# Streaming-window attention with folded feed-forward weights: the casting queue's gate one piece earlier, paired copies of fold sums, and new numbers in the planner

## The chip, the cores and the metric

The kernel runs on 1 core of one Trainium2 chip. The metric is the device time of one execution in microseconds. Before the change it is 201.57 us, the median of three runs (201.42 to 201.92).

The engines are named as in the profile: PE is TensorE (PEld its weight loads), DVE is VectorE, ACT is ScalarE, POOL is GpSimd and SP is SyncE. SP and POOL issue nearly all transfers here: SP plain copies and transposing copies, POOL those that cast from float32 to bfloat16 on the way.

## What is computed

Attention with 4 sink keys and a window of 128 keys over 4 batches, 8 heads, 768 positions and 64 dimensions, followed by a gated feed-forward block whose last two matrices follow each other with nothing between them:

```python
scores = scale * q @ k.transpose(0, 1, 3, 2)
keep = is_sink | in_window            # 4 sinks; 0 <= i - j < 128
a = softmax(where(keep, scores, -1e9))
x = (a @ v)  as [3072, 512]
out = ((x @ w1) * (x @ w2)) @ w3 @ w_out
```

`w1` and `w2` are 512 x 1024, `w3` is 1024 x 1024 and `w_out` is 1024 x 512.

## The kernel before

**Folding.** The product `w3 @ w_out` doesn't depend on the tokens. The kernel works it out once, as `w3o`, in 8 row blocks of 128: `fold_w3` transposes a row block of `w3` on PE (line 403) and DVE copies the result (line 408), `fold_mm` multiplies it with `w_out` on PE (line 433) in four steps of two column blocks each, and ACT copies the finished sum of 128 x 512 from PSUM into `w3o` (line 437). For row blocks 0 to 3 the sums of a pair (0 and 1, 2 and 3) are the two halves of one PSUM tile `ph`, taken from the pool that the attention scores use too (`ps_sc`, two buffers); row blocks 4 to 7 have a tile `pw` each.

**Loading.** Nine pieces of `w3` and `w_out` of 512 KB each come uncast over SP's queue, straight away (`raws`, line 155), into memory that is used for other things later; DVE or ACT casts each of them (line 413). All else comes through POOL's queue: for batch 0 the keys, queries and values, one row block of 128 positions at a time (line 108), two more pieces of `w3` (line 115), and `w1` and `w2` in quarters (line 111). This queue is held back: POOL first copies one column of the piece `casts[hold - 1]` into `spent` (line 190), so it can't issue a load before that piece has landed. In POOL's order the copy stands after the masks and before all loads. With `hold = 6` it is the sixth piece. The loads of batches 1 to 3 are emitted later, when the planner has all folding done.

**Attention.** For each batch, keys and queries are transposed: on PE for batches 0 and 1 (line 200, copied by DVE in line 202), by transposing copies on SP's queue for batches 2 and 3 (line 207). PE works out scores (lines 256 and 277), ACT the exponentials (lines 261 and 281), DVE applies the mask, PE multiplies with the values (lines 309 and 346), DVE divides, and the result is transposed into `xT`, on PE or, for batches 2 and 3, by copies on SP's queue (line 373).

**Feed-forward.** `gate` multiplies `xT` with `w1` and with `w2` on PE (line 386); ACT copies the first product (line 393) and DVE multiplies the second into it (line 390). `project` multiplies with `w3o` (line 444), ACT copies (line 448) and SP writes the result out (line 451). A batch's gates come in chunks of 256 tokens for batch 0 and of 384 for the others, 8 column blocks each.

**The order of the work.** The order of instructions on PE, ACT, DVE and SP is made in Python before anything runs. Each piece of work is a `task` with a priority, a cost for each stage, and the tasks, loads and PSUM buffers that it waits for. `landings` works out when each load lands: `RAW` is when SP's queue begins to move data, `DGE` the time from POOL's issue to the first data, the third number of an entry the lag from the last data to the landing. `service` gives, for each load of POOL's queue, the time that POOL takes to issue it and the time that its data take. `landings` counts `spent` as passed 0.3 us after the held piece lands, keeps eight of POOL's loads in flight, and shares the DMA engines by fixed numbers while both queues have work: for small attention loads, 0.79 of full speed to the uncast pieces and 0.13 to the others. A loop then picks the next instruction of each engine by these times. `PACE` is the shortest time, for each batch, between the starts of two pairs of score units. `keep_busy` puts matmuls on zeros (line 458) where PE would otherwise stand in the first 40 us of the plan. Once made, each engine's order is fixed: an instruction whose input is late holds up all that stand behind it on its engine.

Of the kernel before, what the change touches and what calls it, by code (L numbers as in the profile page):

```python
# [21 lines left out]
def kernel(  # L22
# [13 lines left out]
    nc = tc.nc  # L36
# [14 lines left out]
    KFF = DF // P  # L51

    CHUNKS = [[(256 * i, 256 * i + 256) for i in range(3)]] + [[(0, 384), (384, 768)]] * (B - 1)
    XPOSE = (2, 3)
# [23 lines left out]
    w3o = wp.tile([P, KFF, DM], BF16, name="w3o")  # L78
# [39 lines left out]
    def load(what, *i):  # L118
# [9 lines left out]
        else:  # L128
            for dst, src in ((w1_sb, moe_w1), (w2_sb, moe_w2)):
# [3 lines left out]
    raws = [("w3", 0, 0, "dve"), ("wo", 0, 0, "act"), ("w3", 2, 0, "dve"), ("wo", 2, 0, "act"),  # L133
            ("w3", 4, 0, "dve"), ("wo", 4, 0, "act"), ("w3", 0, 1, "dve"), ("wo", 6, 0, "act"),
            ("w3", 2, 1, "dve")]
    hold = 6

    order = [("qkv", 0, 0, 1), ("w3", 4, 1, 2), ("qkv", 0, 1, 2), ("w3", 6, 0, 2), ("qkv", 0, 2, 3),
             ("qkv", 0, 3, 4), ("w12", 0, 1), ("w12", 1, 2), ("w12", 2, 3), ("w12", 3, 4), ("qkv", 0, 4, 5),
             ("qkv", 0, 5, 6), ("qkv", 1, 0, 6), ("qkv", 2, 0, 6), ("qkv", 3, 0, 6)]  # L140
# [258 lines left out]
    def fold_w3(i, j0, j1):  # L399

        tp = ps_mm.tile([P, j1 - j0, P], BF16, tag="mm", name="tp3")
        for j in range(j0, j1):
            nc.tensor.transpose(tp[:, j - j0, :], w3_sb[:, i, j * P:(j + 1) * P], ident)
        yield
        if i not in w3T:
            w3T[i] = (flat((kN, qN)[i - 4][1], "k s")[:, 2048:3072].rearrange("p (k n) -> p k n", n=P)
                      if i in (4, 5) else work.tile([P, KFF, P], BF16, tag="w3t", bufs=4, name="w3t"))
        nc.vector.tensor_copy(w3T[i][:, j0:j1, :], tp[:])
        yield
# [6 lines left out]
    held = {}  # L416
    FM = [[(0, 2), (2, 4), (4, 6), (6, KFF)] for i in range(KFF)]

    def folded(i):
        return ("fm", i, len(FM[i]) - 1)  # L420

    def fold_mm(i, j0, j1):

        if i >= 4:
            if j0 == 0:
                held[i] = ps_mm.tile([P, DM], FP32, tag="mm", name="pw")
            po = held[i][:]
        else:
            if i % 2 == 0 and j0 == 0:
                held[i // 2] = ps_sc.tile([P, 2, DM], FP32, tag="sc", name="ph")  # L430
            po = held[i // 2][:, i % 2, :]
        for j in range(j0, j1):
            nc.tensor.matmul(po, w3T[i][:, j, :], wo_sb[:, j, :],  # L433
                             start=(j == 0), stop=(j == KFF - 1))
        yield
        if j1 == KFF:
            nc.scalar.copy(w3o[:, i, :], po)  # L437
        yield

    def project(b, m, n0, n1):  # L440

# [20 lines left out]

    def service(what, *i):
        if what == "qkv":
            return [(0.87, 0.845 + (1.2 if i[0] in XPOSE and x != "v" else 1.3 if (x, *i) == ("v", 0, 4, 5) else 0.0), [(x, i[0], kb)])
                    for kb in range(i[1], i[2]) for x in "kqv"]
        if what == "w3":
            return [(0.75, 1.3 * (i[2] - i[1]), [("w3", i[0], h) for h in range(i[1], i[2])])]
        if what == "wo":
            return [(0.81, 0.65 * (i[1] - i[0]), [("wo", x, 0) for x in range(i[0], i[1], 2)])]  # L470
        return [(0.8, 1.34 * (i[1] - i[0]), [(w,) + (n,) for n in range(i[0], i[1])]) for w in ("w1", "w2")]

    def landings(RAW=2.0, POOL=3.0, DGE=1.6, RAMP=(0.33, 0.64, 0.66, 0.9)):

        queues = {"sp": [(RAW, 1.31, 1.0, [("raw",) + x[:3]]) for x in raws],
                  "pool": [(gen, us, 1.9, keys) for x in order for gen, us, keys in service(*x)]}
        left = {n: [us for _, us, _, _ in q] for n, q in queues.items()}
        at = {n: 0 for n in queues}
        landed, issue, ready, now = [], POOL, [], 0.0
        while any(at[n] < len(q) for n, q in queues.items()):  # L480
            while len(ready) < len(queues["pool"]) and (len(ready) < 8 or len(landed) > len(ready) - 8) \
                    and at["sp"] >= hold:
                if not ready and hold:
                    issue = max(issue, arrive[("raw",) + raws[hold - 1][:3]] + 0.3)
                if len(ready) >= 8:
                    issue = max(issue, landed[len(ready) - 8])
                issue += queues["pool"][len(ready)][0]
                ready.append(max(5.8, issue + DGE))
            busy = [n for n, q in queues.items() if at[n] < len(q)
                    and now >= (q[at[n]][0] if n != "pool" else ready[at[n]] if at[n] < len(ready) else 1e9)]  # L490
            small = queues["pool"][at["pool"]][3][0][0] if "pool" in busy else ""
            for n in busy:
                i = int(now - RAW) if now >= RAW else 0
                share = 1.0 if len(busy) == 1 else 0.5 if small not in "kqv" else 0.79 if n == "sp" else 0.13
                left[n][at[n]] -= 0.02 * share * (RAMP[i] if i < len(RAMP) else 1.0)
                if left[n][at[n]] <= 0.0:
                    lag, keys = queues[n][at[n]][2:]
                    for key in keys:
                        arrive[key] = now + lag
                    if n == "pool":  # L500
                        landed.append(now + lag)
                    at[n] += 1
            now += 0.02

    landings()

    tasks = {}
# [3 lines left out]
    def task(name, prio, gen, stages, after=(), loads=(), ring=None, started=(),  # L511
             half=False, slots=1, paced=False):
        tasks[name] = dict(name=name, prio=prio + nudge.get(name, 0.0), gen=gen, stages=stages, after=list(after),
                           loads=list(loads), ring=ring, started=list(started), half=half,
                           slots=slots, paced=paced)
# [6 lines left out]
    def need(what, i, h):  # L522
        key = (what, i // 2 * 2, h)
        return ([("c",) + key], []) if key in raw_keys else ([], [key])

    for i in range(KFF):
        for h in range(2):
            j0, j1 = 4 * h, 4 * h + 4
            needs = [need("w3", i, x) for x in range(j0 // 4, j1 // 4)]
            task(("t3", i, h), 100 + i + (5 if i < SPLIT and h else 0), fold_w3(i, j0, j1),  # L530
                 [("pe", 0.055 * (j1 - j0)), ("dve", 0.05 + 0.075 * (j1 - j0))],
                 [x for a, _ in needs for x in a], [x for _, a in needs for x in a],
                 started=[("t3", i, 0)] if i >= SPLIT and h else [folded(i - SPLIT)] if i >= SPLIT else [], ring="mm")
        for h, (j0, j1) in enumerate(FM[i]):
            last = j1 == KFF
            begin = i < 4 and i % 2 == 0 and h == 0
            needs = [need("wo", x, 0) for x in range(j0, j1, 2)]
            task(("fm", i, h), 100.5 + i + (5 if i < SPLIT and j0 >= 4 else 0) + 0.1 * h, fold_mm(i, j0, j1),
                 [("pe", 0.216 * (j1 - j0))] + ([("act", 0.6)] if last else []),
                 [("t3", i, 1 if j0 >= 4 else 0)] + ([("fm", i, h - 1)] if h else [])  # L540
                 + [x for a, _ in needs for x in a],
                 [x for _, a in needs for x in a],
                 "sc" if begin else "mm" if i >= 4 and h == 0 else None,
                 started=[("fm", i - 1, 0)] if i < 4 and not begin and h == 0 else [])
            if last and (i % 2 or i >= 4):
                tasks["fm", i, h]["frees"] = ("fm", i if i >= 4 else i - 1, 0)
# [70 lines left out]
    for b in range(B):  # L617
        for c, (t0, t1) in enumerate(CHUNKS[b]):
            last_t = (t1 - 1) // 256
            us = 0.01 + 0.65 * (t1 - t0) / 384  # L620
# [21 lines left out]
    MARGIN = {"av": 0.3}  # L642

    YIELD = {"g": 0.0, "av": 0.0, "sc": 0.4, "tdk": 1.5, "tdq": 1.5}
    PACE = [0.0, 3.2, 4.5, 5.0]
    last_sc = 0.0
    START, WARM_UNTIL = 1.2, 40.0
    BACKLOG = 1.6
# [12 lines left out]
    def pe_pick():  # L661
        best = None
        for k in tasks.values():
# [16 lines left out]
            if k["paced"]:  # L680
                busy = max(0.0, free["act"] - free["pe"]) + sum(q[2] for q in queue["act"])
                est = max(est, free["pe"] + busy - BACKLOG, last_sc + (PACE[k["name"][1]]))
            wait = est - free["pe"]
# [32 lines left out]
    while len(done) < len(tasks):  # L716
# [4 lines left out]
        for k in tasks.values():  # L721
            e, us = k["stages"][0]
# [5 lines left out]
        pe = pe_pick()  # L728
# [9 lines left out]
        if e == "pe":  # L738
# [8 lines left out]
            us = k["stages"][0][1]  # L747
# [5 lines left out]
        else:  # L753
            q = picks[e]
            queue[e].remove(q)
            us, k = q[2], q[3]
# [37 lines left out]
```

## Time and profile before

| | us |
|---|---|
| median of three runs | 201.57 |
| the profiled execution | 200.9 |
| its span, first to last instruction | 199.2 |
| DVE busy | 111.1 |
| ACT busy | 107.9 |
| POOL busy | 75.6 |

The granted PE clock was 0.998 of full speed over the span. A row of the timeline gives the start in us from the start of the span, the length, engine, line, operation, output and inputs, the number of instructions merged into the row, and in brackets how long the engine stood before it and what released it. A row of the chain of waits gives start, length and what. A row of a table by stretches gives the stretch, its length, and for each engine its busy time and number of instructions, then the granted clock, the DMA share and GB/s.

### The profile page before, as it was taken

The page shows a single profiled execution, that of the slowest core. Times are in us where ns is not written, and L with a number is a line of the kernel's source. Part 1 is how long each engine was busy: PE and PEld are TensorE (multiplying, and loading weights), DVE is VectorE, ACT ScalarE, POOL GpSimd, SP SyncE. Part 2 cuts the span into 40 slices and gives each one's busy share as a digit, 9 for nine tenths or more (in the row PEclk, how much of TensorE's full clock was granted, in tenths as well). Part 3 has the DMA queues.
Part 4 walks back from the last instruction along what each step waited for, and adds up shares of the span by engine and source line. Part 5 has one row for each costly group of instructions (what it writes and reads, how often), then busy time and mean ns, then how long its engine had stood idle before and what let it go on. Part 6 is the DMA issues. An engine that isn't in the chain of part 4 may idle for free.

```text
span 199.2 us, 4550 instructions
## 1 busy us (share of the span) xinstructions
PE 192.8 (97%) x1815; PEld 119.2 (60%) x1815; DVE 111.1 (56%) x262; ACT 107.9 (54%) x181; POOL 75.6 (38%) x102
## 2 busy tenths in 40 slices
PE   7999899999999999999999999999999999999993
PEld 2445465889866887665656655665664465554442
DVE  5555487756589778677768656767751044440000
ACT  2234576843767877866775656766622433333332
POOL 5149978679899954545374200000000000000000
PEclk9999999999999999999999999999999999999999
DMA  4999999999999999999999999960505410002333
GB/s 148 382 389 152 173 159 192 195 169 153 155 150 180 198 162 111 148 172 164 131 153 147 131 156 179 219 64 0 56 0 161 155 56 2 0 0 104 143 142 141
DMA packets 105301, 28.35 MB, mean 142 GB/s; under 512 B 95168, under 2 KB 99776, under 8 KB 105280
## 3 DMA queue, kind: packets, MB, share of 16 engines
q0 software_dynamic: 79648, 12.33, 87.2%
q1 hardware_dynamic: 25488, 15.60, 38.0%
q8 instruction: 14, 0.23, 0.5%
q10 hardware_dynamic: 144, 0.13, 0.2%
q14 instruction: 7, 0.06, 0.1%
HBM read 29.36 MB, written 6.29 MB: 179 GB/s over the span
## 4 chain that ended last, share of the span: by engine, by line
PE 85%; DMA 8%; POOL 3%; SPq 1%; DVE 1%; ACT 1%; issue 0%
PE pg L386 43%; PE po L444 21%; PE av L346 6%; PE sc L256 5%; DMA ab<-in_moe_w_out_dram 4%; DMA qN<-in_q_dram 3%; PE tp L200 3%; PE pw L433 2%; SPq L155 1%; POOL kN L108 1%; PE xt L362 1%; PE av L309 1%; PE sp L237 1%; PE sc L277 1%; POOL qN L108 1%; ACT ex L281 1%
## 5 line engine op out<-in xcount | busy, mean ns | idle before, releaser
L386 PE MATMUL pg<-xT,w_sb 128*128 128x384 bf16 (+1 forms) x576 | 92.4, 308 | 0.0
L386 PEld LDWEIGHTS <-w_sb 128*128 128x128 bf16 x576 | 52.7, 98 | 24.7 <-issue 1.6
L390 DVE TENSOR_TENSOR ab<-a_sb,pg 128x384 bf16<-128x384 f32 (+1 forms) x72 | 36.6, 509 | 36.5 <-PE pg L386 31.8
L393 ACT COPY a_sb<-pg 128x384 f32<-128x384 f32 (+1 forms) x72 | 32.0, 445 | 35.0 <-PE pg L386 17.3
L444 PE MATMUL po<-w3o,ab 128*128 128x512 bf16 (+1 forms) x200 | 43.1, 371 | 0.0
L261 ACT ACTIVATE ex<-sc 128x1024 bf16<-128x1024 f32 (+1 forms) x40 | 37.4, 963 | 5.7 <-PE sc L256 4.1
L444 PEld LDWEIGHTS <-ab 128*128 128x128 bf16 x200 | 19.1, 98 | 20.6 <-issue 0.5
L448 ACT COPY w_sb<-po 128x512 f32<-128x512 f32 (+1 forms) x25 | 14.2, 569 | 25.9 <-PE po L444 25.8
L108 POOL DMA_DIRECT2D qN<-in_q_dram x24 | 22.2, 923 | 11.2 <-DMA vN<-in_v_dram 8.6
L265 DVE TENSOR_TENSOR am<-ex,maskt 128x1024 bf16<-128x1024 bf16 (+1 forms) x40 | 25.4, 645 | 1.3 <-ACT ex L261 1.0
L108 POOL DMA_DIRECT2D kN<-in_k_dram x24 | 22.4, 933 | 7.6 <-DMA qN<-in_q_dram 4.6
L108 POOL DMA_DIRECT2D vN<-in_v_dram x24 | 21.7, 904 | 6.4 <-DMA kN<-in_k_dram 5.0
L353 DVE TENSOR_TENSOR xn<-av,rec 128x256 bf16<-128x256 f32 x40 | 17.0, 425 | 1.4
L346 PE MATMUL av<-vN,am 128*128 128x65 bf16 x296 | 16.2, 193 | 0.0
L346 PEld LDWEIGHTS <-am 128*128 128x128 bf16 x296 | 14.0, 97 | 2.3
L350 DVE RECIPROCAL rec<-av 128x4 f32<-128x4 f32 x40 | 7.1, 179 | 10.4 <-PE av L346 10.3
L256 PE MATMUL sc<-kqT 64*128 64x128 bf16 (+1 forms) x216 | 11.6, 238 | 0.0
L202 DVE COPY kqT<-tp 128x1024 bf16<-128x1024 bf16 x12 | 8.3, 691 | 5.4 <-PE tp L200 5.3
L346 PE MATMUL av<-vs,es 128*128 128x130 bf16 x56 | 11.1, 220 | 0.0
L256 PEld LDWEIGHTS <-kqT 64*128 64x128 bf16 x216 | 6.9, 94 | 4.0 <-issue 3.2
L281 ACT ACTIVATE ex<-sc 128x1024 bf16<-128x1024 f32 x7 | 7.2, 1031 | 2.9 <-PE sc L277 2.8
L433 PE MATMUL ph<-wo_sb,w3t 128*128 128x512 bf16 x32 | 7.9, 380 | 0.7 <-ACT w3o L437 0.3
(68 smaller groups left out, 138.2 us busy)
## 6 DMA issues: line engine op xcount, KB each, us to landing
out_dram<-w_sb SPq DMA_DIRECT2D x23, 256.0 KB, 2.2
kN<-in_k_dram POOLq DMA_DIRECT2D x24, 128.0 KB, 7.9
qN<-in_q_dram POOLq DMA_DIRECT2D x24, 128.0 KB, 8.1
vN<-in_v_dram POOLq DMA_DIRECT2D x24, 128.0 KB, 7.9
w_sb<-in_moe_w_dram POOLq DMA_DIRECT2D x9, 256.0 KB, 8.3
ab<-in_moe_w_dram SPq DMA_DIRECT2D x3, 512.0 KB, 6.5
ab<-in_moe_w_out_dram SPq DMA_DIRECT2D x3, 512.0 KB, 7.4
kN<-in_moe_w_dram SPq DMA_DIRECT2D x1, 512.0 KB, 9.4
```

The lines of the kernel that those rows point to most:

```text
L108: nc.gpsimd.dma_start(out=dst, in_=rows(src, b, kb))
L256: nc.tensor.matmul(sc[:, e, c:c + n], kT[b][hp, r, kb * P:(kb + 1) * P], qT[b][hp, r, qb * P:qb * P + n], start=True, stop=True)
L261: nc.scalar.activation(ex[:, :, c0:], sc[:, :, c0:], ACTF.Exp, scale=scale)
L265: nc.vector.tensor_mul(am[:, :, c0:], ex[:, :, c0:], mk)
L346: nc.tensor.matmul(o, lhs, rhs, start=(n == 0), stop=(n == len(todo) - 1), skip_group_check=True)
L353: nc.vector.tensor_mul(xns[b, t][:, :, r, :, :], av[:, :, :, 0:D], rec[:].to_broadcast([P, 2, 2, D]))
L386: nc.tensor.matmul(pg[:], w_sb[:, kk, dt * P:(dt + 1) * P], xT[b][:, kk, tk], start=(kk == 0), stop=(kk == NP - 1))
L390: nc.vector.tensor_mul(ab[b][:, dt, tk], gate_a.pop((b, c, dt))[:], pg[:])
L393: nc.scalar.copy(a_sb[:], pg[:])
L433: nc.tensor.matmul(po, w3T[i][:, j, :], wo_sb[:, j, :], start=(j == 0), stop=(j == KFF - 1))
L444: nc.tensor.matmul(po[:], ab[b][:, kk, m * P:(m + 1) * P], w3o[:, kk, n0:n1], start=(kk == 0), stop=(kk == KFF - 1))
L448: nc.scalar.copy(o_sb, po[:])
```

## The change

The gate `spent` reads the fifth uncast piece, not the sixth. For row blocks 0 to 3 the copy of a finished sum is done once for a pair: the even row block has no copy, and the odd one copies both halves of the tile, 128 x 1024, to `w3o`; its last step is made to wait for the last step of the even row block in the plan. Row blocks 4 to 7 are as before. The rest are numbers of the planner: the issue time of batch 0's attention loads, the extra time of one of them, the start and the lag of POOL's loads, the cost of the paired copy, and the pacing of batches 1 to 3.

```diff
-    hold = 6
+    hold = 5
...
-        if j1 == KFF:
+        if j1 == KFF and i >= 4:
             nc.scalar.copy(w3o[:, i, :], po)
-        yield
+            yield
+        elif j1 == KFF and i % 2:
+            nc.scalar.copy(w3o[:, i - 1:i + 1, :], held[i // 2][:])
+            yield
...
-            return [(0.87, 0.845 + (1.2 if i[0] in XPOSE and x != "v" else 1.3 if (x, *i) == ("v", 0, 4, 5) else 0.0), [(x, i[0], kb)])
+            return [(0.95 if i[0] == 0 else 0.87, 0.845 + (1.2 if i[0] in XPOSE and x != "v" else 0.7 if (x, *i) == ("v", 0, 4, 5) else 0.0), [(x, i[0], kb)])
...
-    def landings(RAW=2.0, POOL=3.0, DGE=1.6, RAMP=(0.33, 0.64, 0.66, 0.9)):
+    def landings(RAW=2.0, POOL=3.0, DGE=1.3, RAMP=(0.33, 0.64, 0.66, 0.9)):
...
-                  "pool": [(gen, us, 1.9, keys) for x in order for gen, us, keys in service(*x)]}
+                  "pool": [(gen, us, 2.2, keys) for x in order for gen, us, keys in service(*x)]}
...
-                 [("pe", 0.216 * (j1 - j0))] + ([("act", 0.6)] if last else []),
+                 [("pe", 0.216 * (j1 - j0))] + ([("act", 0.6 if i >= 4 else 1.04)] if last and (i % 2 or i >= 4) else []),
                  [("t3", i, 1 if j0 >= 4 else 0)] + ([("fm", i, h - 1)] if h else [])
+                 + ([("fm", i - 1, h)] if last and i < 4 and i % 2 else [])
...
-    PACE = [0.0, 3.2, 4.5, 5.0]
+    PACE = [0.0, 3.4, 5, 4.5]
```

## The prediction

> **What bounds the kernel now.** I read the engine table first, then the stretches, then the chain of waits, then the first 45 us row by row.
>
> ```profile
> PE 192.8 (97%) x1815; PEld 119.2 (60%) x1815; DVE 111.1 (56%) x262; ACT 107.9 (54%) x181; POOL 75.6 (38%) x102
> ...
> 30.00:35.00 5.00, 5.00 (x68) 2.84 (x67) 3.53 (x7) 3.25 (x5) 3.88 (x6) 1.00 1.57 193
> ...
> 120.00:150.00 30.00, 30.00 (x301) 18.23 (x298) 20.36 (x47) 18.22 (x30) 0.00 (x0) 1.00 0.66 83
> ```
>
> The second number of a stretch is TensorE's busy time. From 30 us on, the stretches before the tail (all quoted or like the two here) have no idle TensorE at all, so after that point the end can come earlier only if TensorE has got through more of its work by then. That leaves the start, where the chain of waits runs through transfers:
>
> ```profile
> 3.54 8.87 DMA ab<-in_moe_w_out_dram
> 12.89 0.80 POOL kN L108
> 13.69 1.27 POOL qN L108
> 17.84 6.29 DMA qN<-in_q_dram
> 24.17 0.40 PE tp L200 x4
> 28.78 0.65 PE tp L200 x8
> ```
>
> The columns are start, length and what. The sixth uncast weight piece lands at 12.41 (3.54 + 8.87); only then does POOL issue the loads of batch 0. The queries of the second row block, issued at 17.84, land at 24.13 and TensorE's transposes stand waiting for them. From 28.78 the chain is TensorE alone.
>
> The same start by stretches of 1 us; the last three columns are granted clock, DMA share and GB/s:
>
> ```profile
> 14.00:15.00 1.00, 1.00 (x8) 0.42 (x7) 0.84 (x3) 0.00 (x0) 1.00 (x2) 1.00 1.06 382
> 15.00:16.00 1.00, 1.00 (x9) 0.55 (x8) 0.66 (x2) 0.86 (x1) 1.00 (x2) 1.00 1.85 223
> 16.00:17.00 1.00, 1.00 (x6) 0.45 (x5) 0.49 (x2) 0.19 (x1) 1.00 (x2) 1.00 2.25 143
> 18.00:19.00 1.00, 0.70 (x8) 0.34 (x6) 0.76 (x2) 0.97 (x2) 1.00 (x2) 1.00 1.34 143
> 19.00:20.00 1.00, 1.00 (x18) 0.81 (x17) 0.31 (x1) 0.00 (x0) 1.00 (x2) 1.00 0.94 92
> 20.00:21.00 1.00, 1.00 (x8) 0.34 (x10) 0.38 (x1) 0.60 (x2) 1.00 (x2) 1.00 1.74 134
> 21.00:22.00 1.00, 0.66 (x10) 0.30 (x6) 0.00 (x0) 1.00 (x2) 1.00 (x2) 1.00 2.33 157
> 22.00:23.00 1.00, 0.72 (x10) 0.45 (x8) 0.46 (x2) 0.98 (x2) 1.00 (x3) 1.00 1.98 185
> 23.00:24.00 1.00, 0.83 (x6) 0.42 (x6) 0.89 (x2) 0.00 (x0) 1.00 (x2) 1.00 1.51 196
> 24.00:25.00 1.00, 0.83 (x11) 0.59 (x12) 0.39 (x1) 0.00 (x0) 1.00 (x2) 1.00 1.21 201
> 28.00:29.00 1.00, 0.89 (x17) 0.74 (x15) 0.95 (x6) 1.00 (x2) 0.81 (x2) 1.00 2.44 155
> 33.00:34.00 1.00, 1.00 (x18) 0.67 (x18) 1.00 (x3) 0.95 (x2) 0.71 (x2) 1.00 1.45 197
> ```
>
> Two things are to be seen. TensorE's idle time is 0.30 us at 18, and 0.34 + 0.28 + 0.17 + 0.17 + 0.11 = 1.07 us between 21 and 29. And the DMA engines, at 382 GB/s with the uncast pieces and 143 to 157 GB/s with small casting loads, fall to 92 GB/s at 19: with POOL busy throughout (1.00) issuing, the casting queue has run short.
>
> **The change, part by part.** These rows carry the terms:
>
> ```profile
> 11.07 0.69 DVE L413 CAST w_sb<-ab 128x1024 bf16<-128x1024 f32 x1 [0.76 <-DMA ab<-in_moe_w_dram]
> 12.46 0.19 POOL L190 COPY spent<-ab 128x1 f32<-128x1 f32 x1 [6.90 <-DMA ab<-in_moe_w_out_dram]
> 16.67 0.69 DVE L413 CAST w_sb<-kqT 128x1024 bf16<-128x1024 f32 x1 [0.51 <-DMA kqT<-in_moe_w_dram]
> 17.48 0.65 PEld L403 LDWEIGHTS <-w_sb 128*128 128x128 bf16 x8
> 20.99 0.59 ACT L437 CAST w3o<-ph 128x512 bf16<-128x512 f32 x1 [0.38 <-PE ph L433]
> 21.63 0.59 PE L433 MATMUL ph<-wo_sb,w3t 128*128 128x512 bf16 x2 [0.34 <-ACT w3o L437]
> 22.10 0.62 PE L403 MATMUL tp<-shifts,w_sb 128*128 128x128 bf16 x8
> 22.39 0.59 ACT L437 CAST w3o<-ph 128x512 bf16<-128x512 f32 x1
> 24.17 0.40 PE L200 MATMUL tp<-shifts,qN 128*128 128x128 bf16 x4 [0.33 <-DMA qN<-in_q_dram]
> 25.49 0.40 PE L277 MATMUL sc<-kqT 64*128 64x128 bf16 x8
> 25.93 1.02 ACT L281 ACTIVATE ex<-sc 128x1024 bf16<-128x1024 f32 x1 [0.30 <-PE sc L277]
> ```
>
> *The gate on the casting queue.* POOL's copy `spent` now reads the fifth piece. VectorE's cast at 11.07 was released by that piece's landing, POOL's copy at 12.46 by the sixth's: 12.46 - 11.07 = 1.39 us. Behind the copy stand, on POOL, the memset of `vN` and every casting load of batch 0 and of the second weights; all move up together, and no waiting instruction is put in front of anything else. But the DMA engines are not free to use it. The first keys, issued until 13.69, show in the rates at about 15 (382 to 223 GB/s); they will show at about 13.6, and until about 15.6 the uncast pieces still need the engines. Busy engines don't move more for being asked earlier. What can be won is the hole at 18 to 21, where nothing was queued. Against 143 GB/s, the rate beside it, it is (143 - 92)/143 + (143 - 134)/143 = 0.42 us; against 197 GB/s, which a stream of weights reaches at 33, it is (197 - 143)/197 + (197 - 92)/197 + (197 - 134)/197 = 1.13 us. Part of what moves there is a weight piece, so I take 0.8 us for everything that the casting queue brings from 20 us on: the queries at about 23.3 instead of 24.13. The ends are 0.4 and, were the whole head start kept, 1.39.
>
> The wait for those queries is 0.33 us in the row. TensorE's times hold a pipeline's end besides: eight transposes take 0.62, four 0.40, so one more costs 0.055 and the end, 0.40 - 4 x 0.055, is 0.18. A wait that goes saves that end too: 0.33 + 0.18 = 0.51 us, and 0.8 covers it. **Term: -0.51**; its ends are 0 (a reordered TensorE meets the next late transfer there) and -0.51.
>
> *What pays for it.* The pieces after the fifth share the engines with the casting loads for some 2.0 us (13.6 to 15.6) instead of 0.6. No row shows such a mixture for long: in the mixed stretch at 15 to 16, 223 GB/s moved, between the two pure rates. At one end the pieces lose nothing, at the other half their rate, 1.4 us for the added 1.4 us of sharing. I take a quarter of those 1.4 us, 0.35 us, nearer the low end because the mixed stretch still moves 80 GB/s more than the casting loads do alone at 16. The last piece, then cast at 16.67 to 17.36 and its transposes loaded from 17.48, had 0.12 us in hand; TensorE stands 0.35 - 0.12 = 0.23 us longer. **Term: +0.23**, ends 0 and +1.28.
>
> The Trainium skill, DMA: Bandwidth & Descriptors, section "Queues, rings and completion order", speaks against the gate's move: each DMA engine takes turns between queues packet by packet. If a turn were one descriptor of a 2 KB piece against one of a 256 B row, an estimate from that rule gives the casting queue a ninth of the bytes during the 2.0 us, so 0.2 us of head start and no more, and the pieces lose about as much; the sum by it would be 0.1 better than mine, and with the whole head start and no loss 0.23 better. No run here yet shows the long mixture.
>
> *The paired copies.* For row blocks 0 to 3, two ScalarE copies of 128x512 at 0.59 become one of 128x1024; the nearest row of that size out of PSUM is the exponential's 1.02, and the planner books 1.04. ScalarE saves 2 x 0.59 - 1.04 = 0.14 us per pair, which is worth nothing by itself at 54% busy. But in the second pair the matmuls of the odd row at 21.63 stood 0.34 us for the even row's copy (20.99 + 0.59 = 21.58), since both sums are halves of one tile. That copy is gone, and with it the wait and its pipeline end: 0.34 + 0.18. **Term: -0.52**, ends 0 (TensorE may then stand as much longer before the weight piece at 22.10) and -0.52. The pair's PSUM buffer comes free 0.45 us later (1.04 for 0.59). The next scores that need one are at 25.49, and the pair's last copy here ends at 22.98, so 2.5 us cover it; uncovered it would cost 0.45.
>
> *The planner's numbers* (generation 0.95, lag 2.2, start 1.3, the fifth value block 0.7, pacing 3.4, 5 and 4.5) are no work on the chip; they change the order in which engines' programs are written. After 30 us TensorE has no idle time to lose, so a new order is worth zero there at best, and a wait at worst; see the rivals.
>
> *The cap.* The first gate matmuls follow the loads of w1 and w2 closely:
>
> ```profile
> 39.17 0.88 POOL L108 DMA_DIRECT2D qN<-in_q_dram  x1 [0.45 <-DMA w_sb<-in_moe_w_dram]
> 40.48 0.88 POOL L108 DMA_DIRECT2D vN<-in_v_dram  x1 [0.44 <-DMA w_sb<-in_moe_w_dram]
> ...
> 42.88 1.75 PE pg L386 x16
> ...
> 157.89 20.80 PE pg L386 x128
> ```
>
> POOL is released there by the landings of these weights, 1.31 us apart; the kernel's model has eight loads in flight, so the piece behind the wait at 40.48 is the sixth of eight, and the eighth lands, by an estimate from that step, at 40.48 + 2 x 1.31 = 43.1. The last 16 of the 64 gate matmuls need it and the seventh from 42.88 on, the w2 half from about 43.3. TensorE can be early there by 0.2 us plus what the stream gains: 0.6 to 1.3 us, 1.0 with my 0.8. My sum stays just below it.
>
> **Sum.** -0.51 + 0.23 - 0.52 = -0.80 us. The profiled execution took 200.9 us with a span of 199.2, 1.7 around it; the span becomes 198.4 and that execution 200.1. The median of the three runs, 201.57, is 0.67 above the profiled one, and I carry the difference over: 201.57 - 0.80 = **200.8 us**.
>
> **Rivals.**
>
> *Nothing, 201.4.* The gate buys only the low end, 0.4 us, and TensorE, free sooner from folding, stands at the second weight piece or at the gate weights of 43 us instead. For it: the cap, and the DMA engines being full but for the hole. Against it: the 0.34 us behind the copy needs no transfer. With 0.4 + 0.2 as the cap and half of it lost to a late last piece, the gain is about 0.2.
>
> *Slower, 202.2: the third tile of batch 3 is asked for before its transposed queries are there.*
>
> ```profile
> 114.89 0.44 PE sc L256 x8
> 135.98 0.55 PE sc L256 x12
> ...
> 125.96 1.67 SPq L207 DMA_TRANSPOSE kqT<-qN  x1
> ...
> DMA to landing us min/median/max: 4.3/8.5/10.1
> ```
>
> Its first pair of scores starts at 135.98, four pairs after 114.89, 5.27 apart under a floor of 5.0. With 4.5 it would come at about 114.89 + 4 x 4.77 = 134.0. The last transpose, issued at 125.96, lands by the median at 134.5 and at the latest at 136.1. TensorE works in order, so all gates behind the scores would wait 0.5 to 2.1 us; at 1.4, with the gain of 0.8 kept, the time is 202.2. It decides from a lead of more than 1.5 us over the old order. Against it: batch 2's floor goes up by as much, from 4.5 to 5, which moves batch 3's start back, and a planner that knows the transposes would put gates first.
>
> *More, 199.9.* All idle time at 21 to 29 goes: 1.07 visible and five waits' pipeline ends, of which four can be taken whole, 4 x 0.18: 1.8 us, less the last piece's 0.23, would be 1.6. It needs the cap at its upper end, and the copies behind each fold transpose to be hidden too.
>
> *The change doesn't do what it says*: were the casting loads issued earlier but landed no earlier, the row at 24.17 would keep its wait; that is part of "nothing".
>
> **How the numbers follow.** Forecast 0.42, with a range of its own from 200.2 to 201.1; more 0.08; nothing 0.26; slower 0.24, in which I put, beside the transposes, any other wait that the new order makes after 30 us. A measurement of this kernel tells about 0.3%, 0.6 us, from no change. So faster 0.50, same 0.26, slower 0.24. The range of 8 in 10 runs from 200.0, most of the larger gain, to 202.2, the slower case at its price.
>
> **What would show it.** Right: `spent` at about 11.1; no stretch below 130 GB/s at 17 to 21; the row-block-1 query transposes at or before 23.5 with no DMA wait; one copy of 128x1024 per pair and no matmul waiting for it; idle TensorE between 21 and 29 halved; a last gate stage as long as now (20.80 us). Wrong: the last uncast piece's cast later than 17.3, or any stretch after 30 us with idle TensorE, above all a score waiting for a transpose near 134 or a gate for a weight near 42.

## The result, and the profile after

The changed kernel takes 200.19 us (median of 8 runs, 199.81 to 200.35) against 201.59 for the one before (8 runs beside it, 200.60 to 202.68). The ratio is 0.9938 with a 95% interval of 0.9915 to 0.9961: 1.25 us faster, 0.8 to 1.7 by the interval. (The two medians lie 1.40 us apart; the text below goes by the ratio.) The forecast of 0.80 us sits at the interval's near edge. The profiled execution took 200.22 us with a span of 198.5.

First the timeline of the kernel after, the rows that answer to those of before:

```profile
10.88 0.69 DVE L413 CAST w_sb<-ab 128x1024 bf16<-128x1024 f32 x1 [0.77 <-DMA ab<-in_moe_w_dram]
10.91 0.71 POOL L190 COPY spent<-ab 128x1 f32<-128x1 f32 x1 [5.38 <-DMA ab<-in_moe_w_dram]
...
16.47 0.69 DVE L413 CAST w_sb<-kqT 128x1024 bf16<-128x1024 f32 x1 [0.50 <-DMA kqT<-in_moe_w_dram]
...
18.09 1.01 ACT L440 CAST w3o<-ph 128x1024 bf16<-128x1024 f32 x1 [2.09 <-PE ph L433]
...
23.20 0.39 PE L200 MATMUL tp<-shifts,qN 128*128 128x128 bf16 x4
```

The gate opens with the fifth piece (10.91 for 12.46). The last uncast piece is not late: its cast starts at 16.47, 5.59 us after the fifth piece's; before the change it was 16.67, 5.60 us after. A pair of sums is copied at once in 1.01 us, as costed from the exponential's row. The query transposes of the second row block run at 23.20 and wait for nothing; before, they stood until 24.17.

The stretches of the kernel after (granted clock, DMA share and GB/s are the last three columns):

```profile
14.00:15.00 1.00, 1.00 (x8) 0.43 (x7) 0.84 (x3) 0.05 (x1) 1.00 (x2) 1.00 1.07 378
15.00:16.00 1.00, 1.00 (x10) 0.52 (x8) 0.63 (x2) 0.99 (x1) 1.00 (x2) 1.00 1.99 213
16.00:17.00 1.00, 1.00 (x6) 0.39 (x4) 0.53 (x1) 0.00 (x0) 1.00 (x2) 1.00 2.43 155
17.00:18.00 1.00, 1.00 (x10) 0.55 (x9) 0.51 (x2) 0.00 (x0) 1.00 (x2) 1.00 2.15 171
18.00:19.00 1.00, 1.00 (x9) 0.51 (x7) 0.50 (x2) 0.91 (x1) 1.00 (x2) 1.00 1.39 194
19.00:20.00 1.00, 1.00 (x12) 0.56 (x11) 0.34 (x1) 0.10 (x1) 1.00 (x2) 1.00 2.17 159
20.00:21.00 1.00, 0.84 (x16) 0.53 (x18) 0.35 (x1) 0.58 (x2) 1.00 (x3) 1.00 2.47 170
```

The hole is gone: 159 GB/s at 19 where 92 stood. But at 14 the engines still run at the rate of the uncast pieces, 378 GB/s, as before the change (382); the casting loads, issued a little over a us earlier, show in the rates no earlier than then, from 15 on. The one stretch of before that the prediction left out moved as much as its neighbours:

```profile
17.00:18.00 1.00, 1.00 (x10) 0.60 (x9) 0.36 (x1) 0.11 (x1) 1.00 (x2) 1.00 2.15 143
```

So from 16 to 21 us the five stretches add up to 655 KB before the change and 849 KB after it. The 194 KB more are 1.1 us at 170 GB/s. Somewhat over half of them (103 KB) move after 19 us, in the hole; the others come from higher rates at 16 to 19.

How far the whole stream of loads moved is read from POOL's waits for landings of `w1` and `w2`, the same loads as in the prediction's rows at 39.17 and 40.48:

```profile
37.87 0.87 POOL L108 DMA_DIRECT2D qN<-in_q_dram  x1 [0.45 <-DMA w_sb<-in_moe_w_dram]
39.17 0.87 POOL L108 DMA_DIRECT2D vN<-in_v_dram  x1 [0.43 <-DMA w_sb<-in_moe_w_dram]
```

They come 1.30 and 1.31 us earlier. About 0.2 of that is this execution's own earlier transfers (the fifth piece's cast, which no edit touches, starts at 10.88 for 11.07), which leaves 1.1 us. The other profiles agree: from the start of that cast to the first of these two rows it is 27.9 to 28.4 us in the four kernels with the gate at the sixth piece, and 26.9 to 27.3 in the eight profiles with the gate at the fifth.

TensorE by coarse stretches, first before, then after:

```profile
18.00:21.00 3.00, 2.71 (x32) 1.48 (x31) 1.45 (x3) 1.56 (x4) 3.00 (x4) 1.00 1.34 123
21.00:30.00 9.00, 7.92 (x98) 4.94 (x95) 6.10 (x18) 5.59 (x8) 7.55 (x10) 1.00 2.04 170
40.00:46.00 6.00, 6.00 (x70) 5.40 (x68) 3.71 (x10) 2.72 (x7) 4.68 (x7) 1.00 2.21 165
```

```profile
18.00:21.00 3.00, 2.84 (x34) 1.59 (x34) 1.19 (x3) 1.59 (x3) 3.00 (x5) 1.00 2.01 175
21.00:30.00 9.00, 8.34 (x114) 5.30 (x112) 6.59 (x19) 5.73 (x9) 7.48 (x10) 1.00 1.98 170
40.00:46.00 6.00, 5.39 (x53) 4.30 (x51) 2.83 (x7) 2.21 (x7) 4.14 (x7) 1.00 2.39 158
```

TensorE's idle time from 18 to 30 us falls from 0.29 + 1.08 = 1.37 to 0.16 + 0.66 = 0.82 us, and 114 matmuls run from 21 to 30 where 98 ran. Some of it comes back as a new wait at 40 to 46, which the timeline places:

```profile
43.37 0.40 PE L200 MATMUL tp<-shifts,kN 128*128 128x128 bf16 x4 [0.23 <-DMA kN<-in_k_dram]
44.14 0.40 PE L200 MATMUL tp<-shifts,qN 128*128 128x128 bf16 x4 [0.38 <-DMA qN<-in_q_dram]
```

TensorE is done with the first gates sooner and stands for the fifth row block's keys and queries. In the chain of waits the last 128 gate matmuls begin at 157.22 and last 20.80 us, as before the change, when they began at 157.89.

### The profile page after: what moved, and what is told of

Read it like the earlier page. It is cut to its first block, busy times and chain, and to the rows that moved or that the text cites. A ratio compares the mean times of both kernels' runs of the same rounds, so it can differ in the third digit from the quotient of the medians.

```text
span 198.5 us, 4533 instructions
## 1 busy us (share of the span) xinstructions
PE 190.3 (96%) x1803; PEld 118.9 (60%) x1815; DVE 111.8 (56%) x262; ACT 107.8 (54%) x179; POOL 75.9 (38%) x102
## 4 chain that ended last, share of the span: by engine, by line
PE 76%; DMA 17%; POOL 4%; SPq 1%; issue 1%; ACT 0%
PE pg L386 39%; PE po L447 21%; DMA w_sb<-in_moe_w_dram 7%; PE av L346 6%; DMA qN<-in_q_dram 5%; PE sc L256 5%; DMA ab<-in_moe_w_dram 4%; PE tp L200 2%; POOL qN L108 1%; POOL vN L108 1%; PE xt L362 1%; SPq L155 1%; POOL kN L108 1%; PE sp L237 1%; PE vp L226 1%
## 5 line engine op out<-in xcount | busy, mean ns | idle before, releaser
L346 PE MATMUL av<-vN,am 128*128 128x65 bf16 x296 | 16.8, 193 | 0.0
```

The lines of the kernel that those rows point to most:

```text
L346: nc.tensor.matmul(o, lhs, rhs, start=(n == 0), stop=(n == len(todo) - 1), skip_group_check=True)
```

## The experiments

Two theories were on the table. One: the gate's move fills the hole in the casting queue, and that is the gain, with the copies worth about as much. The other: the new order of instructions is what gained. Every ratio below is to the kernel before on the same chip, with its 95% interval.

**The gate alone.** POOL reads another piece and the plan knows nothing of it, so every engine's order is the one of before.

```diff
-        nc.gpsimd.tensor_copy(spent[:], casts[hold - 1][1][:, 0, 0:1])
+        nc.gpsimd.tensor_copy(spent[:], casts[4][1][:, 0, 0:1])
```

> The kernel before with one edit: POOL's gate reads the fifth uncast piece; the order on every engine is the one of before. Theory (the hole in the casting queue): no rate below 130 GB/s between 17 and 21 us, the queries of row block 1 land 0.8 to 1.2 us earlier, their wait (0.33 us) goes, and the time falls by 0.4 to 0.9 us (ratio 0.9955 to 0.998). Rival (the order is what gained): with the old order the engines wait elsewhere instead, ratio 0.9985 to 1.0015.

Measured: 200.08 us, ratio 0.992 (0.9894 to 0.9947). It is the whole gain, and more than the expected range. The stretch at 19 us is back at 156 GB/s, and the wait for the even row's copy, on which the prediction spent 0.52 us, still stands in its timeline:

```profile
19.00:20.00 1.00, 0.84 (x15) 0.61 (x14) 0.69 (x1) 0.37 (x1) 1.00 (x3) 1.00 2.27 156
```

```profile
21.23 0.59 PE L433 MATMUL ph<-wo_sb,w3t 128*128 128x512 bf16 x2 [0.34 <-ACT w3o L437]
```

So neither the copies nor the new order are needed for the gain. The rival of the order falls.

**The gate undone.** The same edit the other way: the changed kernel, its order unchanged, with `casts[5]`.

> The changed kernel with one edit: POOL's gate reads the sixth piece again, the order on every engine stays the changed one. Theory: the hole is back, the new order meets the loads 1.1 us later than it was made for, and most of the gain is lost: ratio to before 0.997 to 1.003. Rival (order): the gain stays, 0.993 to 0.996.

Measured: 201.6 us, ratio 1.0003 (0.998 to 1.0026). All of the gain is lost, as the theory has it. In its stretches the rate at 19 us is down again, and in its timeline TensorE stands for both of the `w3` pieces that come through the casting queue:

```profile
19.00:20.00 1.00, 1.00 (x17) 0.58 (x15) 0.50 (x1) 0.00 (x0) 1.00 (x3) 1.00 1.21 127
```

```profile
21.52 0.62 PE L403 MATMUL tp<-shifts,w_sb 128*128 128x128 bf16 x8 [0.43 <-DMA w_sb<-in_moe_w_dram]
...
26.64 0.57 PE L403 MATMUL tp<-shifts,w_sb 128*128 128x128 bf16 x7 [0.93 <-DMA w_sb<-in_moe_w_dram]
```

The changed kernel, with the same order, keeps one such wait, of 0.31 us:

```profile
25.70 0.84 PE L403 MATMUL tp<-shifts,w_sb 128*128 128x128 bf16 x12 [0.31 <-DMA w_sb<-in_moe_w_dram]
```

The gate's move thus takes 0.43 + 0.93 - 0.31 = 1.05 us of waiting from TensorE here. How far ahead it stays can be read from ScalarE, which runs the same instructions in the same order in both kernels; an exponential and the last copy, first with the gate undone, then changed:

```profile
30.64 1.02 ACT L281 ACTIVATE ex<-sc 128x1024 bf16<-128x1024 f32 x1 [2.31 <-PE sc L277]
...
196.37 0.37 ACT L451 COPY w_sb<-po 128x256 f32<-128x256 f32 x1 [0.46 <-PE po L447]
```

```profile
29.67 1.02 ACT L281 ACTIVATE ex<-sc 128x1024 bf16<-128x1024 f32 x1 [2.11 <-PE sc L277]
...
195.34 0.37 ACT L451 COPY w_sb<-po 128x256 f32<-128x256 f32 x1 [0.46 <-PE po L447]
```

The lead is 0.97 us at the first and 1.03 at the second.

**The copies alone.** The kernel before with the edit of `fold_mm` and its two planner lines from the change.

> The kernel before with the paired copies and their cost in the plan, and nothing else. Theory (the term of -0.52): the wait of 0.34 us for the even row's copy goes and the time falls by 0.2 to 0.5 us (ratio 0.9975 to 0.999). Rival: TensorE reaches the next weight piece at 22.1 us earlier and waits as much longer there, ratio 0.999 to 1.001; a new order can add a wait and go to 1.003.

Measured: 201.4 us, ratio 0.9997 (0.9969 to 1.0024). The value is the first rival's; the interval still holds the theory's 0.2 to 0.5 us. The wait for the even row's copy is gone, and TensorE waits for loads instead. Its table of waits:

```profile
PE tp L403 <- DMA w_sb<-in_moe_w_dram: 1.0, 1, 1.0
PE tp L200 <- DMA qN<-in_q_dram: 0.9, 1, 0.9
PE sp L237 <- DMA kqT<-qN: 0.9, 1, 0.9
```

```profile
27.13 0.84 PE L403 MATMUL tp<-shifts,w_sb 128*128 128x128 bf16 x12 [0.99 <-DMA w_sb<-in_moe_w_dram]
45.76 0.40 PE L200 MATMUL tp<-shifts,qN 128*128 128x128 bf16 x4 [0.92 <-DMA qN<-in_q_dram]
125.64 0.29 PE L237 MATMUL sp<-kqT,ksbd 128*32 128x256 bf16 x4 [0.87 <-DMA kqT<-qN]
```

The profiled execution is one of this kernel's longer ones (202.69 us in a range of 200.72 to 203.01). It shows what the profile of before did not: an execution can lose 1.0 us at 27, 0.9 us at 45, and again 0.9 us at 125 us for a transposing copy. That the gate at the sixth piece is to blame for all three isn't shown: the kernel with the gate at the fourth piece (further down) waits 0.87 us for the same queries, at 44.17, and that execution took 200.24 us.

**The planner's numbers alone**, the gate at the sixth piece:

```diff
+ ... (0.95 if i[0] == 0 else 0.87, ... 0.7 if (x, *i) == ("v", 0, 4, 5) else 0.0) ...
...
+ ... DGE=1.3, ...
...
+ ... (gen, us, 2.2, keys) ...
...
+    PACE = [0.0, 3.4, 5, 4.5]
```

> The kernel before with the planner's new numbers (issue times, start, lag, pacing) and nothing else; the gate stays at the sixth piece. Theory: no idle time after 30 us to win, ratio 0.998 to 1.002. Rival (the old numbers cost waits): ratio 0.994 to 0.997, with the waits between 18 and 29 us down by half.

Measured: 201.29 us, ratio 0.9993 (0.9969 to 1.0018). No change that can be told, as the theory has it.

**The fifth row block later on TensorE**, aimed at the wait at 43 to 44 us:

```diff
     landings()
+    for n in "kqv":
+        arrive[n, 0, 4] += 1.0
```

> The changed kernel; the plan is told that the fifth row block of batch 0 lands 1.0 us later, so that two gate products of the second chunk (16 matmuls, 1.75 us) stand ahead of its transposes on TensorE. Nothing else of the order differs. Theory: the waits of 0.23 and 0.38 us for these keys and queries near 43 to 44 us were what the gain still lost, and the end comes 0.5 to 0.9 us earlier than in the changed kernel (ratio to before 0.988 to 0.991). Rival: the row block is needed for the next scores, and the wait turns up behind them, ratio 0.992 to 0.996.

Measured: 199.83 us, ratio 0.9931 (0.9906 to 0.9956), in the rival's range. The wait at 43 is gone; in its timeline another stands at the transposes of a later row block:

```profile
57.56 0.40 PE L200 MATMUL tp<-shifts,qN 128*128 128x128 bf16 x4 [0.40 <-DMA qN<-in_q_dram]
```

**The old pacing** in the changed kernel, `PACE = [0.0, 3.2, 4.5, 5.0]`:

> The changed kernel with the old pacing 3.2, 4.5 and 5.0. Theory: TensorE has no idle time there either way, ratio to before 0.992 to 0.996 like the changed kernel. Rival: the new pacing was a part of the gain, 0.996 to 1.0.

Measured: 199.93 us, ratio 0.9938 (0.9912 to 0.9965). The pacing is worth nothing that can be told.

**The gate much earlier.** The changed kernel with the gate at the first piece (`casts[0]`), and with the gate at the fourth (`casts[3]`), to see what a longer head start brings and who pays.

> The changed kernel with the gate at the first uncast piece (about 5.5 us), the order unchanged. Theory from the four runs so far (casting loads move nothing until the uncast pieces are through): the last uncast piece lands as before, the first casting data at about 15 us, no hole, ratio to before 0.990 to 0.995. Rival (the queues share, as the kernel's own model has it, 0.79 to 0.13): the uncast pieces come later, the last one by 1 to 2 us, folding waits, ratio 0.997 to 1.01.

> The changed kernel with the gate at the fourth piece, the order unchanged. Theory: no hole is left to fill, ratio to before 0.991 to 0.996. Rival (every piece of head start is worth about as much as the first): 0.984 to 0.990; rival (sharing): 0.996 to 1.002.

Measured: 200.21 us, ratio 0.997 (0.9944 to 0.9996) at the first piece; 200.18 us, ratio 0.9949 (0.9923 to 0.9975) at the fourth. A further piece of head start brings nothing more that can be told; of four more, the value is the near end of the rival's range, and the interval reaches from the gain of the fifth to almost none. The rival's mechanism, which the theory denied, is in the profile. The gate at the first piece, stretch and timeline, and the packets from 14 to 15 us by queue (q1 is SP's, q0 POOL's; count, MB, share of 16 engines):

```profile
14.00:15.00 1.00, 0.60 (x6) 0.23 (x4) 0.99 (x2) 0.00 (x0) 0.00 (x0) 1.00 1.22 325
```

```profile
6.14 1.04 POOL L108 DMA_DIRECT2D kN<-in_k_dram  x1
...
17.81 0.94 POOL L108 DMA_DIRECT2D kN<-in_k_dram  x1 [4.18 <-DMA kN<-in_k_dram]
```

```profile
17.57 0.69 DVE L413 CAST w_sb<-kqT 128x1024 bf16<-128x1024 f32 x1 [1.19 <-DMA kqT<-in_moe_w_dram]
```

```profile
q1 hardware_dynamic: 160, 0.31, 90.9%
q0 software_dynamic: 158, 0.02, 30.6%
```

Now the queues do share: 325 GB/s at 14 us for 378, and the last uncast piece is cast at 17.57 for 16.47, 1.1 us late. And the casting loads get little by it: of 0.33 MB in that us, 0.02 are theirs, and POOL's ninth load is released at 17.81 by the landing of the first keys, which it had begun to issue at 6.14. This bears out the Trainium skill, DMA: Bandwidth & Descriptors, section "Queues, rings and completion order", by which each DMA engine takes turns between queues packet by packet: the two queues move as many packets, 160 and 158, and the one with the small rows so gets about a sixteenth of the bytes. The profile counts a casting load as it is written, in bfloat16 (128 KB for the 128 x 512 keys of a row block); by the float32 that is read it is twice as much, the ninth that the prediction estimated. With the gate at the fifth piece the sharing is hardly to be seen: from 14 to 15 us the casting queue moves 26 packets beside 194.

**Four on one chip**: the changed kernel again, the later row block again, the later row block with the old pacing, and the kernel before with the gate at the fifth piece and the paired copies, under the old numbers.

> The changed kernel itself, on one chip with the three that follow, so that they can be compared with it: 199.9 to 200.3 us, ratio to before 0.992 to 0.995.

> The changed kernel with the fifth row block's transposes two gate products later on TensorE. Theory (the wait near 43 us is what the end still loses): 0.3 to 0.6 us under the changed kernel of this job. Rival (the wait turns up at a later row block): within 0.15 us of it.

> Both the later transposes and the old pacing 3.2, 4.5 and 5.0. Theory: the pacing is worth nothing, so the same as the run with the later transposes alone, within 0.2 us. Rival: the old pacing is better, 0.3 us or more under it.

> The kernel before with the gate at the fifth piece and the paired copies, planned with the old numbers. Theory after the runs with one part each: the gate carries all, the copies nothing: ratio to before 0.991 to 0.995, as for the gate alone. Rival (the copies' wait of 0.34 us counts once the loads are early): 0.988 to 0.9905.

Measured, in that order: 199.97 us, 0.9942 (0.9919 to 0.9964); 200.07 us, 0.9939 (0.9914 to 0.9964); 199.44 us, 0.9933 (0.9912 to 0.9955); 199.55 us, 0.9949 (0.992 to 0.9978). The intervals lie on one another, so the later row block is worth nothing that these runs can tell, nor is any of the other three shown to beat the changed kernel; the copies add nothing to the gate. One point stays open: the old pacing on top of the later row block has a median 0.63 us under that of the later row block alone, which is the rival's range, but by the ratios the two are only 0.0006 apart, 0.1 us. The second profile of the changed kernel says why the wait at 43 us was no handle:

```profile
42.89 0.39 PE L200 MATMUL tp<-shifts,kN 128*128 128x128 bf16 x4
43.24 0.40 PE L200 MATMUL tp<-shifts,qN 128*128 128x128 bf16 x4
```

The same program doesn't wait there in this execution, and that took 199.94 us, where the one with the waits took 200.22.

## Why the prediction was right, and which terms were not

**The hole in the casting queue was the cause**, as the first part had it. Gate alone, 0.992; gate undone, 1.0003; the copies and the planner's numbers, each alone, move nothing that can be told. No stretch is below 159 GB/s from 17 to 21 us, and the wait of 0.33 us for the queries is gone. But the 0.8 us for the stream was too little: it came 1.1 us earlier, at the prediction's weight-rate end (1.13).

**The 0.80 us came out partly by luck.** It lies within the measured interval, but two of its three terms were wrong, and the -0.29 us that they add up to brought the sum nearer to the 1.25 us measured. The time, 200.19 us, lies just beyond the fast end of the forecast's own range, 200.2 to 201.1.

**"+0.23 for what pays" was wrong in this place.** It took the uncast pieces to lose a quarter of the added sharing. They lost nothing with the gate at the fifth piece, since the casting data hardly flowed earlier at all: the prediction had them show at 13.6, 1.4 us earlier than before, and they showed at about 15 as before. The cost exists, though, with the gate at the first piece: the last uncast piece 1.1 us later.

**"-0.52 for the paired copies" was wrong.** The mechanism is real: the wait is there without the copies and gone with them. But with the gate at the sixth piece TensorE then waits at a landing (0.99 us at 27.13), the zero end of that term. With the gate at the fifth, gate and copies (0.9949, from 0.992 up) are no better than the gate alone (0.992), and the range that went with the term, 0.988 to 0.9905, lies outside the interval. What the runs favour for the term is 0.

**"-0.51 for the queries' wait" was too small for the gate.** With the other two terms at 0, the sum would have been -0.51 against 1.25 measured. The missing part is that I priced one wait for a landing, where every later load has the same 1.1 us more in hand: in the changed order it is the waits for the two weight pieces that shrink, by the 1.05 us worked out above. The argument that nothing can be won after 30 us came from one execution of before, in which TensorE does not idle there. That execution, at 200.9 us, was among the faster ones: beside the last four runs the kernel before ran from 200.16 to 202.90 us in 28 runs, the changed kernel from 199.35 to 200.63 in 12. The one long execution that was profiled with the gate at the sixth piece, that of the copies alone, has its waits for loads at 27, 45 and 125 us. That the kernel before loses its 202 us at these places was not profiled and stays open. How much is won before 30 us differs between the profiled pairs. With the gate undone against the changed kernel, nearly all of the lead is there by 31 us (0.97 of 1.03). So it is with the kernel before against the gate alone (exponentials at 31.53 and 30.84, last copies at 196.01 and 195.23: 0.69 of 0.78), but there the last uncast `w_out` piece was already cast 0.41 us earlier (15.14 and 14.73), ahead of anything that the gate does. With the copies alone against gate and copies (31.36 and 29.96, 197.83 and 194.41) it is 1.40 of 3.42, the long execution against a short one. For the medians the split stays open.

**The cap** was right in kind: the new wait at 43 to 44 us, 0.61 us of idle time at 40 to 46, is TensorE ahead of the loads, at the fifth row block's keys and queries and not at a gate weight. Idle time after 30 us was among the signs of being wrong. It varies between executions of one program, and moving the work behind it moved no time.

**The rivals.** "Slower", by the transposed queries of batch 3, did not come with the new pacing; a like wait, 0.87 us at 125 us, did come in the kernel with the copies alone, under the old pacing. "Nothing" is out by the interval. "More" comes as near in size as the forecast (its gain is 1.6 us, and 201.57 less 1.6 is 200.0, not the 199.9 at its head), but not in kind: of the 1.08 us of idle time at 21 to 29, 0.66 stay, so it isn't halved either.

## What to carry to other kernels

A gate on a queue of small loads is worth moving only as far as the queue runs dry behind it: look for the stretch in which the DMA rate falls while the issuing engine is busy, fill it, and stop; here, further head start brought nothing or took from the loads in front. Where, as here, many steps wait for the same stream of loads, removing one engine's wait between two landings was worth nothing, and moving the stream was worth more than the one wait that had been priced. One profiled execution without idle time doesn't show that the next has none: compare the spread of the runs before writing a stage off.

## What the hardware did that was not expected

While the uncast pieces were queued, a casting load showed in the rates long after its issue. With the gate at the fifth piece the first one's issue ends at 12.67 (the gate's copy at 10.91, then 11.63 for 1.04), and at 14 us the engines still move 378 GB/s, the rate of the uncast pieces alone; with the gate at the first piece, keys issued from 6.14 have their first packets between 10 and 11 us and landed at 17.8. The head start of 1.5 us at the gate, 1.0 at the first issue, thus bought hardly any earlier data, only a queue that no longer ran dry four us later.

POOL's copy for the gate took 0.71 us where it took 0.19 before. It now starts at 10.91, within VectorE's cast of 10.88 to 11.57, and ends with it (11.62). That VectorE's cast holds it up is how I read these two rows; it wasn't tested by itself, but other profiles fit: with the gate alone the copy takes 0.71 us again, from 10.70 under a cast at 10.67, and with the gate at the fourth piece, where no such cast runs, 0.19.
